# A gated mix of attention and a state-space convolution, backward pass: parameters prepared beside the projections, short-lag kernel gradient taken into the main channel loop

## The chip, the cores and the metric

The kernel runs on one core of one Trainium2 chip. The core has TensorE (PE, with its weight loads shown apart as PEld), VectorE (DVE), ScalarE (ACT), GpSimd (POOL) and SyncE (SP), which here issues the DMA transfers, in program order. The metric is the device time of one execution in microseconds (us), as the median of several runs.

## The reference

The reference computes the forward output and the gradients of all twelve differentiable inputs of a gated mix of two branches, for x of shape 1 x 2048 x 576:

```python
g = sigmoid((x * gate_w).sum(-1, keepdims=True))
a = attention(x, wqkv, wo)           # 32 heads of 18, softmax
# state-space branch, for each of 576 channels d with 128 states n:
dt = exp(log_dt)[:, None]
logdA = dt * (A_re + 1j * A_im)
P = exp(logdA[:, :, None] * arange(2048))
K = einsum("dn,dnl,dn->dl", Cc, P, dt * Bc).real
y = causal_convolution(x, K) + x * Dskip      # by FFT, length 4096
out = g * a + (1 - g) * y
out, vjp = jax.vjp(...); grads = vjp(grad_out)
```

Inputs and outputs are bf16.

## The kernel before

The sequence of 2048 tokens is 16 blocks of 128 (NB = 16), the 576 channels are five pieces of up to 128 (`dch`). The kernel has stages that follow one another:

- **Projections** (L84 to L212). x is transposed, q, k and v are projected for groups of four heads (`ps_proj`), scaled and stored. SyncE makes four transposes of `d_a` (the output gradient times the gate) for all 16 token tiles at L161. A loop over the 16 tiles (L201 to L212) then multiplies by wo transposed (`ps_dO`, ten matmuls) and evicts on VectorE and ScalarE in turn. `ps_dO` has one PSUM buffer.
- **Attention**, forward and backward, 230 to 2657 us, then the weight gradients, to 2870.8 us. The change does not touch them.
- **State-space parameters** (L604 to L720). 16 tiles of x are reversed by a matmul with `J_bf` and stored as `xr_d` (L636 to L643). The six parameter tensors are loaded by channel and transposed on PE (L658). From them come A times dt (`ath_d`, L676), the powers of the transition for a step of 1 and of 128 (`zpow`, L694) and 14 rows per channel, `par_d` (L720).
- **Short-lag kernel gradient** (L722 to L797): the part of dK for lags below 128. It is made from products of x with the gated output gradient inside each 16-token sub-block and up to seven sub-blocks back. For each of three batches of 192 channels, `xs` gets eight copies of x, each shifted by one more 16-token sub-block, by eight loads from DRAM (L765); partitions that would cross a block of 128 are set to zero by a mask (L767). `gyp` is the output gradient times 1 - g (L770), zero in its second half. A unit of 16 channels is 16 matmuls into `psM`, a copy to `mst` (L780), four stores to `Md_d` (L783) and two skewed loads back (`skw`, L789) with a matmul each that sums the diagonals into `dkp`. At the end `dkp` is copied to `DK` and its first row, the gradient of Dskip, to `dDs_d`. `xs`, `gyp` have two buffers each, `mst` three.
- **Main loop** (L799 to L986), 18 blocks of 32 channels; two blocks share what is loaded for 64. `load_rx` (L807) builds `RX`, the right-hand sides: x reversed, the gated gradient, both times their index, and the two columns of `DK`. `egen` (L819), twice per block for 16 channels each, loads `abuf` and `thb` (1 MB each; `thb` has one buffer) and computes the powers `E1e`; a DMA transpose on SyncE makes `E1n` of it (L873). 16 channels' `uvr` and `uvi` matmuls with E1e go to `UV`. VectorE runs a recurrence of 15 steps over the token blocks (`HG`, L888 to L896). GpSimd multiplies by a row of `par` (`wa` L912, `wb` L913, `Rw` L915, VectorE L916). `ybp` matmuls take E1n and Rw. VectorE's products `pA`, `pB`, `pC` (L942) are summed on PE into `smp`, and GpSimd finishes with small operations (L963). The kernel's first 128 lags go through `Kp_d` to `T0w` for the stage `t0_stage` (L841), which runs one block late.
- **Final** (from L988): the parameter gradients from sums over the states, the outputs.

A scheduler sets the order on each engine from the program's order and the buffers. SyncE issues each DMA in its place in that order: if one waits, all behind it wait.

Of the kernel before, what the change touches and what calls it, by code (L numbers as in the profile page):

```python
# [9 lines left out]
A = mybir.AluOpType  # L10
# [10 lines left out]
def build(tc, aps, dbg_aps=None, stages=("s1", "attn", "post", "s4", "final")):  # L21
# [39 lines left out]
    with ExitStack() as gctx:  # L61
# [24 lines left out]

        DPAD = DC * P
# [4 lines left out]
        with ExitStack() as ctx:  # L92
# [36 lines left out]
            go_tok = s1.tile([P, NT, D], BF, name="go_tok1")  # L129
            nc.sync.dma_start(go_tok, go_v)  # L130

# [22 lines left out]
            d_a = s1.tile([P, NT, DPAD], BF, name="d_a1")  # L154
            nc.gpsimd.memset(d_a[:, :, D:DPAD], 0.0)
            for t in range(NT):
                nc.vector.tensor_scalar(d_a[:, t, 0:D], go_tok[:, t, :], g_t[:, t:t + 1], None, op0=A.mult)
            for c in range(DC):
                nc.sync.dma_start_transpose(out=woT[:, :, c * P:(c + 1) * P], in_=wo_pad[:, c, :])
            d_aT = s1.tile([P, NT, DC, P], BF, name="d_aT")  # L160
            for tb in range(NBK):  # L161
                nc.sync.dma_start_transpose(out=d_aT[:, tb * TB:(tb + 1) * TB, :, :].rearrange("p t c q -> p (t c) q"),
                                            in_=d_a[:, tb * TB:(tb + 1) * TB, :].rearrange("p t d -> p (t d)"))

# [36 lines left out]
            for t in range(NT):  # L201
                psd = psB.tile([P, 2, 512], F32, tag="dO", bufs=1, name="ps_dO")
                for u, (f0, fsz) in enumerate(HALF):
                    for c, (e0, esz) in enumerate(dch):
                        mm(psd[:, u, 0:fsz], lhsT=d_aT[0:esz, t, c, :], rhs=woT[0:esz, c, f0:f0 + fsz],
                           start=(c == 0), stop=(c == DC - 1))
                dO_t = work.tile([P, D], BF, tag="dO_t", bufs=3, name="dO_t")
                if t % 2 == 0:
                    nc.vector.tensor_copy(dO_t.rearrange("p (u f) -> p u f", u=2), psd[:, :, 0:DH2])
                else:  # L210
                    nc.scalar.copy(dO_t.rearrange("p (u f) -> p u f", u=2), psd[:, :, 0:DH2])
                nc.sync.dma_start(dO_d[:, t, :], dO_t)  # L212

# [368 lines left out]
        if "s4" in stages:  # L582
            A_re = aps["B_A_re"]; A_im = aps["B_A_im"]; B_re = aps["B_B_re"]; B_im = aps["B_B_im"]
            C_re = aps["B_C_re"]; C_im = aps["B_C_im"]; log_dt = aps["B_log_dt"]; Dskip = aps["B_Dskip"]
            N = A_re.shape[1]
            NB = S // P
            NS = NB - 1
            SUB = 16
            NSUB = P // SUB
# [3 lines left out]
            NPAR = 14  # L593
            INV2PI = float(1.0 / (2.0 * np.pi))
            ath_d = dram.tile([2, D, N], F32, name="ath_d")
            par_d = dram.tile([P, NPAR, D], F32, name="par_d")
            omg_d = dram.tile([S], F32, name="omg_d")
            MW = P + SUB
            Md_d = dram.tile([D, SUB, MW], F32, name="Md_d")
            Kp_d = dram.tile([D, 2 * P], BF, name="Kp_d")  # L600
            yd_d = dram.tile([P, 2, NB, D], BF, name="yd_d")
            xr_d = dram.tile([P, NB, D], BF, name="xr_d")

            s4c_cm = tc.tile_pool(name="s4c", bufs=1)  # L604
            s4c = s4c_cm.__enter__()
            dt_b = s4c.tile([P, D], F32, name="dt_b")
            Ar_n = s4c.tile([P, D], BF, name="Ar_n"); Ai_n = s4c.tile([P, D], BF, name="Ai_n")
            Br_n = s4c.tile([P, D], BF, name="Br_n"); Bi_n = s4c.tile([P, D], BF, name="Bi_n")
            Cr_n = s4c.tile([P, D], BF, name="Cr_n"); Ci_n = s4c.tile([P, D], BF, name="Ci_n")
            S0r = s4c.tile([P, D], F32, name="S0r"); S0i = s4c.tile([P, D], F32, name="S0i")  # L610
            S1r = s4c.tile([P, D], F32, name="S1r"); S1i = s4c.tile([P, D], F32, name="S1i")
            DK = s4c.tile([P, 2, D], BF, name="DK")
            dDs_d = dram.tile([1, D], F32, name="dDs_d")
            nident_bf = s4c.tile([P, P], BF, name="nident_bf")
            nc.vector.tensor_scalar(nident_bf, ident_bf, -1.0, None, op0=A.mult)
# [8 lines left out]

            with ExitStack() as ctx:
                pp = ctx.enter_context(tc.tile_pool(name="s4pp", bufs=2))
                pp1 = ctx.enter_context(tc.tile_pool(name="s4pp1", bufs=1))
                pps = ctx.enter_context(tc.tile_pool(name="s4pps", bufs=2, space=bass.MemoryType.PSUM))
                with nc.allow_non_contiguous_dma(reason="gate values regrouped by 16 tokens"):
                    nc.sync.dma_start(omg_d.rearrange("(t p) -> p t", p=P), omg_t)  # L630
                DH2 = D // 2
                for t in range(NB):
                    x_t = pp.tile([P, D], BF, tag="x_t4", name="x_t4")
                    nc.sync.dma_start(x_t, x_v[:, t, :])
                    xr_t = pp.tile([P, D], BF, tag="xr_t4", name="xr_t4")
                    for u in range(2):  # L636
                        psr = pps.tile([P, DH2], F32, tag="psr", name="psr")
                        mm(psr, lhsT=J_bf, rhs=x_t[:, u * DH2:(u + 1) * DH2])
                        if u == 0:
                            nc.vector.tensor_copy(xr_t[:, 0:DH2], psr)  # L640
                        else:
                            nc.scalar.copy(xr_t[:, DH2:D], psr)
                    nc.sync.dma_start(xr_d[:, t, :], xr_t)  # L643
                zero_bf = pp1.tile([P, P], BF, name="zero_bf")
                nc.vector.memset(zero_bf, 0.0)
                for c, (d0, dsz) in enumerate(dch):
                    nc.sync.dma_start(Kp_d[d0:d0 + dsz, 0:P], zero_bf[0:dsz, :])
                tmpb = pp.tile([P, D], BF, tag="rowb", name="rowb")
                nc.sync.dma_start(tmpb, log_dt.rearrange("(o d) -> o d", o=1).to_broadcast([P, D]))
                nc.scalar.activation(dt_b, tmpb, ACT.Exp)  # L650
                cnt = 0
                for src_ap, dst in ((A_re, Ar_n), (A_im, Ai_n), (B_re, Br_n), (B_im, Bi_n), (C_re, Cr_n), (C_im, Ci_n)):
                    blk_ = pp.tile([P, DC, N], BF, tag="pblk", name="pblk")
                    for c, (d0, dsz) in enumerate(dch):
                        nc.sync.dma_start(blk_[0:dsz, c, :], src_ap[d0:d0 + dsz, :])
                    for c, (d0, dsz) in enumerate(dch):
                        pt = pps.tile([P, P], BF, tag="tp", name="pt_par")
                        nc.tensor.transpose(pt[:, 0:dsz], blk_[0:dsz, c, :], ident_bf[0:dsz, 0:dsz])  # L658
                        if cnt % 2 == 0:
                            nc.vector.tensor_copy(dst[:, d0:d0 + dsz], pt[:, 0:dsz])  # L660
                        else:
                            nc.scalar.copy(dst[:, d0:d0 + dsz], pt[:, 0:dsz])
                        cnt += 1
                    if src_ap is A_re or src_ap is A_im:
                        ltc = pp.tile([P, DC], BF, tag="ltc", name="ltc")
                        nc.gpsimd.memset(ltc, 0.0)
                        for c, (d0, dsz) in enumerate(dch):
                            nc.sync.dma_start(ltc[0:dsz, c:c + 1], log_dt.rearrange("(d o) -> d o", o=1)[d0:d0 + dsz, :])
                        dtc = pp.tile([P, DC], F32, tag="dtc", name="dtc")
                        nc.scalar.activation(dtc, ltc, ACT.Exp)  # L670
                        if src_ap is A_im:
                            nc.scalar.mul(dtc, dtc, INV2PI)
                        which_ = 0 if src_ap is A_re else 1
                        for c, (d0, dsz) in enumerate(dch):
                            sc_ = pp.tile([P, N], F32, tag="adn", name="adn")
                            nc.vector.tensor_scalar(sc_[0:dsz, :], blk_[0:dsz, c, :], dtc[0:dsz, c:c + 1], None, op0=A.mult)  # L676
                            nc.sync.dma_start(ath_d[which_, d0:d0 + dsz, :], sc_[0:dsz, :])

                def newt(nm):
                    return pp1.tile([P, D], F32, tag=nm, name=nm)  # L680

                def tt(o, a, b, op):
                    nc.vector.tensor_tensor(o, a, b, op=op)

                Wr_n = newt("Wr_n"); Wi_n = newt("Wi_n"); t1 = newt("t1")
                tt(Wr_n, Cr_n, Br_n, A.mult); tt(t1, Ci_n, Bi_n, A.mult)
# [32 lines left out]
                for r_, s_ in enumerate((Zr_n, Zr_n, Zr_n, Zr_n, Zi_n, Zi_n, nz, nz, wzr, wzi, zr_n, zi_n, nwr, nwi)):  # L719
                    nc.sync.dma_start(par_d[:, r_, :], s_)  # L720
# [447 lines left out]
```

## Time and profile before

| what | us |
|---|---|
| median of 3 runs (4868.92 to 4871.76) | 4869.47 |
| profiled execution | 4874.1 |
| its span | 4872.4 |
| projections, to attention's first matmul | 230.4 |
| start of the parameter stage | 2870.8 |
| start of the short-lag stage (memset of xs) | 2935.6 |
| start of the main loop (first RX load) | 3404.9 |
| first ybp matmul of the main loop | 3498.6 |

All of these are from the trace, but the first. A row of the windows table gives a stretch of the span: its length, the busy time and the number of instructions of each engine, the clock granted to TensorE, the share of time in which the DMA engines worked, and the bytes they moved. A row of the chain gives what ended last at each moment: an engine with its line, a DMA, or an engine's queue ("SPq") issuing. A group's row gives busy time, mean duration of one in ns, the idle time of the engine just before it, and what released it.

### The profile page before, as it was taken

How to read it: one execution, taken by the hardware profiler on the slowest of the kernel's cores; microseconds unless marked ns; L12 is line 12 of the kernel's file. 1: busy time of each engine (PE TensorE's matmuls, PEld its weight loads, DVE VectorE, ACT ScalarE, POOL GpSimd, SP SyncE). 2: the span in 40 equal slices, each digit the busy share in tenths (PEclk: the TensorE clock that was granted, in tenths of full speed). 3: DMA queues.
4: the chain of work that ended last, by engine and by line, in shares of the span. 5: the costliest groups of instructions: out<-in, count | busy, mean ns of one | idle time of the engine just before them, and what ended most of it. 6: DMA issues, size and time to landing. Idle time of an engine off the chain costs nothing. (4 is left out here: it accounts for less than half of the span.)

```text
span 4872.4 us, 64871 instructions
## 1 busy us (share of the span) xinstructions
PE 3174.3 (65%) x24304; PEld 1144.3 (23%) x24304; DVE 3011.4 (62%) x5252; ACT 2883.8 (59%) x5068; POOL 528.1 (11%) x747
## 2 busy tenths in 40 slices
PE   8899999999999999999997870222122122222121
PEld 2222222222222222222222440111122121122110
DVE  4267677776777777777776221001677666667768
ACT  4399899898998989899895110000444433443411
POOL 0000000000000000000000003000243343344320
PEclk9755555555555555555555975555555555555555
DMA  6357767777677676786768752223544544454347
GB/s 172 100 93 125 135 120 125 136 125 135 120 124 139 124 135 120 129 133 120 129 119 164 197 146 86 68 59 76 148 108 102 129 108 114 108 115 114 102 99 177
DMA packets 1761726, 594.16 MB, mean 122 GB/s; under 512 B 1679615, under 2 KB 1732033, under 8 KB 1752195
## 3 DMA queue, kind: packets, MB, share of 16 engines
q1 hardware_dynamic: 1761410, 590.02, 58.8%
q8 instruction: 191, 3.13, 0.3%
q14 instruction: 125, 1.02, 0.1%
HBM read 193.30 MB, written 59.49 MB: 52 GB/s over the span
## 5 line engine op out<-in xcount | busy, mean ns | idle before, releaser
L478 DVE TENSOR_TENSOR ds<-ps_P,PT 128x512 bf16<-128x512 f32 x2048 | 1329.3, 687 | 468.6 <-PE ps_P L30 262.5
L469 ACT ACTIVATE PT<-ps_P 128x512 bf16<-128x512 f32 x2048 | 1226.4, 603 | 138.7 <-PE ps_P L30 86.8
L473 ACT ACTIVATE eb<-ps_P 128x512 bf16<-128x512 f32 x2048 | 1236.1, 605 | 19.9 <-PE ps_P L30 19.4
L30 PE MATMUL ps_P<-dOaT,VaT_g 19*128 19x512 bf16 x2048 | 1197.7, 601 | 27.1 <-DMA VaT_g<-VaT_d 26.2
L30 PE MATMUL ps_P<-KaT_g,QaT_g 19*128 19x512 bf16 x2048 | 1165.4, 593 | 7.6 <-ACT PT L469 7.6
L30 PE MATMUL ps_P<-QaT_g,KaT_g 19*128 19x512 bf16 x2048 | 1053.7, 615 | 10.1 <-DMA KaT_g<-KaT_d 6.1
L30 PE MATMUL uvr<-RX,E1e 128*128 128x64 bf16 x576 | 72.4, 291 | 655.3 <-DVE E1e L834 655.3
L30 PE MATMUL accO<-PT,Vtok_g 128*32 128x512 bf16 x2048 | 331.5, 631 | 0.0
L30 PE MATMUL accK<-dsT,Qtok_g 128*32 128x256 bf16 x4096 | 315.1, 406 | 1.7 <-DVE dqa L355 0.8
L30 PEld LDWEIGHTS <-VaT_g 19*128 19x128 bf16 x2048 | 197.4, 98 | 434.7 <-issue 404.8
L30 PEld LDWEIGHTS <-KaT_g 19*128 19x128 bf16 x2048 | 135.6, 103 | 690.7 <-issue 664.9
L30 PEld LDWEIGHTS <-E1e 128*128 128x128 bf16 x1152 | 119.7, 123 | 731.8 <-DVE E1e L834 636.6
L780 ACT COPY mst<-psM 128x512 f32<-128x512 f32 x36 | 21.9, 609 | 440.3 <-PE psM L30 364.6
L30 PE MATMUL accQ<-ds,Ktok_g 128*32 128x512 bf16 x2048 | 266.9, 620 | 1.2 <-DVE dvacc L338 1.2
L30 PE MATMUL accV<-eb,dOa 128*32 128x512 bf16 x2048 | 267.0, 620 | 0.6 <-DVE dkacc L379 0.6
L499 POOL MEMSET O_tok<- 128x1024 bf16 x1 | 1.0, 957 | 2429.3 <-DMA dqkv_d<-dtk 2429.3
L767 DVE TENSOR_SCALAR xs<-xs,msk 128x3072 bf16<-128x3072 bf16 x21 | 21.4, 1020 | 379.3 <-DMA xs<-in_A_x_dram 379.3
L30 PE MATMUL psM<-xs,gyp 128*32 128x128 bf16 x576 | 54.7, 550 | 261.2 <-DVE xs L767 189.1
L826 ACT ACT_TABLE_LOAD x35 | 44.9, 1283 | 297.1 <-DMA abuf<-ath_d 296.9
L30 PE MATMUL ybp<-Rw,E1n 128*128 128x31 bf16 x1152 | 71.2, 233 | 224.9 <-POOL Rw L915 219.5
L30 PEld LDWEIGHTS <-QaT_g 19*128 19x128 bf16 x2048 | 178.8, 100 | 51.7 <-issue 28.0
L355 DVE TENSOR_TENSOR dqa<-dqa,accQ 128x512 f32<-128x512 f32 x224 | 153.8, 687 | 48.9 <-PE accQ L30 48.6
(300 smaller groups left out, 4436.3 us busy)
## 6 DMA issues: line engine op xcount, KB each, us to landing
abuf<-ath_d SPq DMA_DIRECT2D x36, 1024.0 KB
thb<-ath_d SPq DMA_DIRECT2D x36, 1024.0 KB
T0w<-Kp_d SPq DMA_DIRECT2D x36, 512.0 KB
dsT<-ds SPq DMA_TRANSPOSE x512
dqkv_d<-dtk SPq DMA_DIRECT2D x96, 72.0 KB
dqkv_tok<-dqkv_d SPq DMA_DIRECT2D x1, 6912.0 KB
Md_d<-mst SPq DMA_DIRECT2D x144, 36.0 KB
ga_d<-ga_st SPq DMA_DIRECT2D x16, 288.0 KB
```

Source lines behind the costliest of these rows:

```text
L30: return nc.tensor.matmul(out, lhsT=lhsT, rhs=rhs, start=start, stop=stop, **kw)
L355: nc.vector.tensor_tensor(U["dqa"], U["dqa"], acc, op=A.add)
L469: nc.scalar.activation(U["PT"][i][:, j, :], ps, ACT.Exp)
L473: nc.scalar.activation(e, ps, ACT.Exp)
L478: nc.vector.tensor_tensor(U["ds"][i][:, j, :], ps, U["PT"][i][:, j, :], op=A.mult)
L499: nc.gpsimd.memset(O_tok[:, :, D:DPAD], 0.0)
L767: nc.vector.tensor_scalar(xs[:, dl, :, :], xs[:, dl, :, :], msk[:, dl:dl + 1], None, op0=A.mult)
L780: nc.scalar.copy(mst[:, :, 0:P], psM)
L826: nc.scalar.activation(abuf, abuf, ACT.Exp, scale=l0col)
```

## The change

The parameter stage moves into the projection stage; `xr_d` is made there from `x_pad`, behind the `dO` loop, with the same single PSUM buffer, and a DMA transpose replaces the transposes on PE. The output gradient and `d_aT` are made there for four tiles at a time, with two buffers, instead of for all 16. The short-lag stage is gone. Its work is four functions that the main loop calls for 64 channels at a time, one pair of blocks ahead; the first 64 channels are done ahead of the loop. `xs` is loaded once from DRAM (256 KB) and shifted seven times by DMAs within SBUF. `xs` and `gyp` have one buffer. `dkp` goes straight into `RX`.

Buffers of the loop change with it: `uvr` and `uvi` share three PSUM buffers (two each before), E1n comes in halves of 16 channels with three buffers, `wa` and `wb` take the buffers of `pA` and `pB`, `rr` has one buffer instead of two, and the first kernel block is transposed in f32 into a part of `smp`. The final stage loads `dt_b` and the six parameters (`prm5`) from DRAM.

```diff
+                    go_b = work.tile([P, TB, D], BF, tag="go_b", name="go_b")
+                    nc.sync.dma_start(go_b, go_v[:, t:t + TB, :])
...
+                    d_aT = work.tile([P, TB, DC, P], BF, tag="d_aT", name="d_aT")
+                    nc.sync.dma_start_transpose(out=d_aT.rearrange("p t c q -> p (t c) q"), in_=d_a.rearrange("p t d -> p (t d)"))
...
+            for t in range(NT):
+                psr = psB.tile([P, 2, 512], F32, tag="dO", bufs=1, name="psr")
+                for u in range(2):
+                    mm(psr[:, u, 0:DH2], lhsT=J_bf, rhs=x_pad[:, t, u * DH2:(u + 1) * DH2])
...
+                pr_ = s1.tile([P, DC, P], BF, name=f"prm{r_}")
+                nc.sync.dma_start_transpose(out=pr_, in_=blk_.rearrange("p c n -> p (c n)"))
...
+                nc.sync.dma_start(prm_d[:, r_, :], pr_)
...
-                    for dl in range(NSUB):
-                        nc.sync.dma_start(xs[dl:P, dl, :, :], xsub[0:P - dl, :, d0:d0 + DB])
...
+                def m_load(xb):
...
+                    nc.sync.dma_start(xs[:, 0, :, :], xsub[:, :, d0:d0 + XB])
...
+                    nc.sync.dma_start(gyp[:, 0:SUB, :], gsub[:, :, d0:d0 + XB])
+                    for dl in range(1, NSUB):
+                        nc.sync.dma_start(xs[dl:P, dl, :, :], xs[0:P - dl, 0, :, :])
+                    nc.vector.tensor_tensor(gyp[:, 0:SUB, :], gyp[:, 0:SUB, :], omp.unsqueeze(2).to_broadcast([P, SUB, XB]), op=A.mult)
+                    for dl in range(1, NSUB):
+                        nc.vector.tensor_scalar(xs[:, dl, :, :], xs[:, dl, :, :], msk[:, dl:dl + 1], None, op0=A.mult)
...
+                def m_fin(xb):
...
+                    nc.vector.tensor_copy(dDs_row[:, xb * XB:(xb + 1) * XB], pk[0:1, :])
+                    nc.scalar.copy(RX[:, CDK, :], pk)
+                    nc.vector.tensor_scalar(RX[:, CDK + 1, :], pk, l0col, None, op0=A.mult)
...
+                m_load(0)
+                load_rx(0)
+                for u in range(4):
+                    m_part(0, u)
+                    m_sum(0, u)
+                m_fin(0)
                 for b in range(D // CB):
...
-                        load_rx(d0 // XB)
+                        if nxt < NXB:
+                            m_load(nxt)
...
+                        E1n_h = pw.tile([P, GS, 2, P], BF, tag="E1n", bufs=3, name="E1n")
...
-                            pr = pps.tile([P, NCOL, 8], F32, tag="uvr", bufs=2, name="uvr")
-                            pi = pps.tile([P, NCOL, 8], F32, tag="uvi", bufs=2, name="uvi")
+                            pr = pps.tile([P, NCOL, 8], F32, tag="uv", bufs=3, name="uvr")
+                            pi = pps.tile([P, NCOL, 8], F32, tag="uv", bufs=3, name="uvi")
...
+                    if nxt < NXB:
+                        if b % 2 == 0:
+                            m_part(nxt, 0)
+                            m_part(nxt, 1)
+                        else:
+                            load_rx(nxt)
+                            m_sum(nxt, 0)
+                            m_sum(nxt, 1)
+                            m_part(nxt, 2)
+                            m_part(nxt, 3)
...
-                        wa = pw.tile([P, 2, NS, CB], F32, tag="wa", bufs=1, name="wa")
-                        wb = pw.tile([P, 2, NS, CB], F32, tag="wb", bufs=1, name="wb")
+                        wa = pw.tile([P, 2, NS, CB], F32, tag="pA", bufs=1, name="wa")
+                        wb = pw.tile([P, 2, NS, CB], F32, tag="pB", bufs=1, name="wb")
...
+                    if nxt < NXB and b % 2 == 1:
+                        m_sum(nxt, 2)
+                        m_sum(nxt, 3)
+                        m_fin(nxt)
...
+                dt_b = pf.tile([P, D], F32, name="dt_b5")
+                nc.sync.dma_start(dt_b, dt_d)
+                prm5 = pf.tile([P, 6, D], BF, name="prm5")
+                nc.sync.dma_start(prm5, prm_d)
```

`m_part` and `m_sum` are the old unit of 16 channels (the 16 matmuls, the copy and the four stores; then the two skewed loads with their matmuls), cut in two.

SyncE at the start of the main loop, before: from the first RX load to the first E1n transpose and the second thb load.

```order
L810 DMA RX<-xr_d 128x16x64
L812 DMA gob<-in_grad_out_dram 128x16x64
L868 DMA par<-par_d 128x14x32
L823 DMA abuf<-ath_d 128x2048
L824 DMA thb<-ath_d 128x2048
L823 DMA abuf<-ath_d 128x2048
L868 DMA par<-par_d 128x14x32
L810 DMA RX<-xr_d 128x16x64
L812 DMA gob<-in_grad_out_dram 128x16x64 x2
L873 DMA_TRANSPOSE E1n<-E1e 128x32x128
L824 DMA thb<-ath_d 128x2048
```

The same engine now, the rows just ahead of the first E1n transpose (L784 and L786 are the loads of `m_load`, L788 its shifts, L807 a store of `m_part`, L818 a load of `m_sum`).

```order
L818 DMA skw<-Md_d 128x1x128 x2
L807 DMA Md_d<-mst_39351 16x4x144 x2
L784 DMA xs_39345<-in_A_x_dram 128x16x64
L786 DMA gyp_39347<-in_grad_out_dram 128x16x64
L818 DMA skw<-Md_d 128x1x128 x2
L788 DMA xs_39345<-xs_39345 127x1024
L788 DMA xs_39345<-xs_39345 126x1024
L788 DMA xs_39345<-xs_39345 125x1024
L788 DMA xs_39345<-xs_39345 124x1024
L788 DMA xs_39345<-xs_39345 123x1024
L788 DMA xs_39345<-xs_39345 122x1024
L788 DMA xs_39345<-xs_39345 121x1024
```

The next two rows are E1n and thb: they have moved behind the stores and loads of the first four units and behind the second load with its seven shifts.

SyncE some blocks into the loop, before:

```order
L933 DMA Kp_d<-KT 32x128
L845 DMA T0w<-Kp_d 128x16x128 x2
L868 DMA par<-par_d 128x14x32
L873 DMA_TRANSPOSE E1n<-E1e 128x32x128
L824 DMA thb<-ath_d 128x2048
L823 DMA abuf<-ath_d 128x2048
L873 DMA_TRANSPOSE E1n<-E1e 128x32x128
```

And now:

```order
L963 DMA Kp_d<-KT 32x128
L788 DMA xs_39345<-xs_39345 121x1024
L853 DMA T0w<-Kp_d 128x16x128 x2
L885 DMA par<-par_d 128x14x32
L807 DMA Md_d<-mst_39349 16x4x144
L735 DMA RX<-xr_d 128x16x64
L807 DMA Md_d<-mst_39349 16x4x144 x3
L807 DMA Md_d<-mst_39351 16x4x144 x2
L892 DMA_TRANSPOSE E1n<-E1e 128x32x128
L864 DMA yd_d<-yd 4096x1x64
L832 DMA thb<-ath_d 128x2048
```

Stores of `mst` and shifts of `xs` stand between the loads of a block and its transpose.

ScalarE in the projection stage, before (L181 and L179 evict projections, L194 is a square root):

```order
L181 ACTIVATE stg<-ps_proj,onec 128x512 x6
L179 ACTIVATE stg<-ps_proj 128x512 x2
L194 ACTIVATE sh<-ps_884,kmxg 128x512
L194 ACTIVATE sh<-ps_898,kmxg 128x512
L179 ACTIVATE stg<-ps_proj 128x512 x2
```

And now (L193, L191 and L206 are the same three; L310 and L311 are sines of `zpow`):

```order
L310 ACT_TABLE_LOAD
L310 ACTIVATE gk<-gv 128x576
L191 ACTIVATE stg<-ps_proj 128x512
L206 ACT_TABLE_LOAD
L206 ACTIVATE sh<-ps_872,kmxg 128x512
L206 ACTIVATE sh<-ps_886,kmxg 128x512
L206 ACTIVATE sh<-ps_900,kmxg 128x512
L191 ACTIVATE stg<-ps_proj 128x512
L193 ACTIVATE stg<-ps_proj,onec 128x512
L311 ACT_TABLE_LOAD
L311 ACTIVATE gv<-gv 128x576
```

The activations of the parameters, with loads of their table and back, stand between the square roots and evictions.

More of the change, by code (lines that the diff above doesn't have):

```diff
@@ L204, in build @@
                     for c, (e0, esz) in enumerate(dch):
-                        mm(psd[:, u, 0:fsz], lhsT=d_aT[0:esz, t, c, :], rhs=woT[0:esz, c, f0:f0 + fsz],
+                        mm(psd[:, u, 0:fsz], lhsT=d_aT[0:esz, t % TB, c, :], rhs=woT[0:esz, c, f0:f0 + fsz],
                            start=(c == 0), stop=(c == DC - 1))
@@ new lines, in build @@
+            zero_bf = s1.tile([P, P], BF, name="zero_bf")
+            nc.vector.memset(zero_bf, 0.0)
+            for c, (d0, dsz) in enumerate(dch):
+                nc.sync.dma_start(Kp_d[d0:d0 + dsz, 0:P], zero_bf[0:dsz, :])
+            dt_b = s1.tile([P, D], F32, name="dt_b")
+            tmpb = work.tile([P, D], BF, tag="rowb", bufs=1, name="rowb")
+            nc.sync.dma_start(tmpb, log_dt.rearrange("(o d) -> o d", o=1).to_broadcast([P, D]))
+            nc.scalar.activation(dt_b, tmpb, ACT.Exp)
@@ new lines, in build @@
+            nc.sync.dma_start(dt_d, dt_b)
+            ltc = s1.tile([P, DC], BF, name="ltc")
+            nc.gpsimd.memset(ltc, 0.0)
+            for c, (d0, dsz) in enumerate(dch):
+                nc.sync.dma_start(ltc[0:dsz, c:c + 1], log_dt.rearrange("(d o) -> d o", o=1)[d0:d0 + dsz, :])
+            dtc = s1.tile([P, DC], F32, name="dtc")
+            nc.scalar.activation(dtc, ltc, ACT.Exp)
+            dtci = s1.tile([P, DC], F32, name="dtci")
+            nc.scalar.mul(dtci, dtc, INV2PI)
@@ L582, in build @@
         if "s4" in stages:
[L583 to L589, printed above, removed]
             CB = 32
@@ new lines, in m_part @@
+                def m_part(xb, u):
+                    d0 = xb * XB
+                    xs = xs2[xb % 2]
+                    gyp = gy2[xb % 2]
+                    psM = pps.tile([P, 4, P], F32, tag="psM", name="psM")
+                    for q in range(4):
+                        for g_ in range(4):
+                            dd = u * 16 + 4 * q + g_
+                            mm(psM[32 * g_:32 * (g_ + 1), q, :].rearrange("p (a b) -> p a b", b=SUB), lhsT=gyp[:, :, dd],
+                               rhs=xs[:, :, ::-1, dd], tile_position=(0, 32 * g_))
+                    mst = mst2[u % 2]
+                    nc.scalar.copy(mst[:, :, 0:P], psM)
+                    for g_ in range(4):
+                        dst = Md_d[d0 + u * 16:d0 + (u + 1) * 16].rearrange("(q g) t w -> g t q w", g=4)
+                        nc.sync.dma_start(dst[g_], mst[32 * g_:32 * g_ + SUB, :, :])
@@ new lines, in m_sum @@
+                def m_sum(xb, u):
+                    d0 = xb * XB
+                    if u == 0:
+                        dkps[xb] = pps.tile([P, XB], F32, tag="dkp", name="dkp")
+                    for v in range(2):
+                        o = u * 16 + v * 8
+                        skw = pw.tile([P, P], F32, tag="skw", bufs=3, name="skw")
+                        src = bass.AP(tensor=Md_d.tensor, offset=Md_d[d0 + o:d0 + o + 1, 0:1, SUB - 1:SUB].offset,
+                                      ap=[[SUB * MW, 8], [MW - 1, SUB], [1, P]])
+                        nc.sync.dma_start(skw, src)
+                        mm(dkps[xb][:, o:o + 8], lhsT=skw, rhs=sel)
```

364 lines of the change are left out of this document (157 added, 207 removed).

## The prediction

> **What bounds the kernel now.** I read the page first, then the windows table cut at the borders of the stages, then the chain of waits of the stretch that the change removes.
>
> ```profile
> span 4872.4 us, 64871 instructions
> ```
>
> The profiled execution took 4874.1 us, 1.7 us more than its span, and lies 4.6 us above the median of the three runs (4869.47 us). The sum below starts from 4874.1 and takes 4.6 off at the end.
>
> The windows table (columns: length, busy time and count on PE, PEld, DVE, ACT, POOL, then the clock, the DMA share, GB/s):
>
> ```profile
> 0.00:230.40 230.40, 192.28 (x784) 67.51 (x784) 87.86 (x186) 83.10 (x125) 10.69 (x29) 0.90 0.46 130
> 2870.80:2935.60 64.80, 17.82 (x62) 5.47 (x62) 33.73 (x80) 15.98 (x42) 0.29 (x5) 0.53 0.54 166
> 2935.60:3404.90 469.30, 93.50 (x720) 62.65 (x720) 34.22 (x38) 22.63 (x38) 46.82 (x10) 0.54 0.27 66
> 3404.90:3498.60 93.70, 11.63 (x96) 10.14 (x97) 56.94 (x87) 42.24 (x34) 14.13 (x11) 0.54 0.61 153
> 3640.00:3780.00 140.00, 31.95 (x482) 29.11 (x483) 98.32 (x179) 58.77 (x57) 49.58 (x69) 0.52 0.46 113
> 4708.00:4872.40 164.40, 21.73 (x146) 9.31 (x144) 124.95 (x251) 25.55 (x48) 0.32 (x2) 0.50 0.68 172
> ```
>
> Row 1 is the projection stage: PE is the engine that sets it, ACT and DVE have more than half of it free. Row 2 prepares the state-space parameters, row 3 is the short-lag kernel gradient. In row 3 no engine is busy for a fifth of the time, and the DMA engines work for 0.27 of it: it is waiting. Row 4 runs from the start of the main loop to its first ybp matmul. Row 5 is one steady 64-channel pair of main-loop blocks: DVE is busy 98 of 140 us, nothing is full. From 2870.8 to the first ybp matmul at 3498.6 it is 627.8 us.
>
> What row 3 waits for, in the chain of waits from 2870 to 3500 (start, length, what):
>
> ```profile
> 2935.63 20.50 POOL xs L747
> 2958.08 38.32 SPq L765
> ...
> 3028.33 26.74 DMA xs<-in_A_x_dram
> ...
> 3246.90 76.69 DMA xs<-in_A_x_dram x3
> ```
>
> The shifted loads (eight of about 760 KB for each third of the channels) and SyncE's time to issue them are the stage. After them its units of 16 channels run one behind another.
>
> **The change: what is taken away.** A stretch of 627.8 us is replaced by one that holds only the first 64 channels' gradient and the loop's own start. The price of its pieces comes from these rows, the units first (timeline), then two landings (chain):
>
> ```profile
> 3067.52 1.63 PE L30 MATMUL psM<-xs,gyp 128*32 128x128 bf16 x16 [0.48 <-ACT mst L780]
> ...
> 3068.12 1.88 SPq L783 DMA_DIRECT2D Md_d<-mst  x4
> ...
> 3070.55 1.22 SPq L789 DMA_DIRECT2D skw<-Md_d  x2
> ...
> 3071.30 1.62 PE L30 MATMUL psM<-xs,gyp 128*32 128x128 bf16 x16 [0.89 <-ACT mst L780]
> ```
> ```profile
> 3060.14 2.72 DMA Md_d<-mst
> ...
> 3075.20 2.55 DMA skw<-Md_d
> ```
> ```profile
> L780 ACT COPY mst<-psM 128x512 f32<-128x512 f32 x36 | 21.9, 609 | 440.3 <-PE psM L30 364.6 <-DMA Md_d<-mst 50.5 <-PE dkp L30 25.2
> ```
>
> One unit alone: 1.6 + 0.6 + 1.9 + 2.7 + 1.2 + 2.6 = 10.6 us; units in a row follow each other by 3.8 us (3067.5 to 3071.3). Four take 10.6 + 3 x 3.8 = 22 us.
>
> How the loop starts now, on SyncE and on VectorE:
>
> ```profile
> 3404.90 0.56 SPq L810 DMA_DIRECT2D RX<-xr_d  x1
> ...
> 3411.31 6.10 SPq L810 DMA_DIRECT2D RX<-xr_d  x1
> ...
> 3431.57 4.98 SPq L873 DMA_TRANSPOSE E1n<-E1e  x1
> 3436.64 0.53 SPq L824 DMA_DIRECT2D thb<-ath_d  x1
> ```
> ```profile
> 3408.95 0.47 DVE L815 TENSOR_SCALAR RX<-RX,l1col 128x960 bf16<-128x960 bf16 x1 [3.65 <-DMA RX<-xr_d]
> 3410.75 1.23 DVE L813 TENSOR_TENSOR RX<-gob,omg_t 128x1024 bf16<-128x1024 bf16 x1 [1.33 <-DMA gob<-in_grad_out_dram]
> ...
> 3417.09 1.28 DVE L827 TENSOR_SCALAR uk<-thb,l0col 128x2048 f32<-128x2048 f32 x1 [4.61 <-DMA thb<-ath_d]
> ```
> ```profile
> 3498.60 1.60 PE L30 MATMUL ybp<-Rw,E1n 128*128 128x31 bf16 x26 [12.72 <-POOL Rw L915]
> ```
>
> From the second thb issue (3436.6) to the first ybp it is 62.0 us, and I keep that. In the new order the first E1n and second thb stand behind the whole first gradient block and the shifts of the second. With T = 2870.8: the 2.8 MB up to thb landed in 12.2 us (3404.9 to 3417.1), 230 GB/s; the new xs load has 2.2 MB with and before it (10 us), and the set-up of masks and zeros stands ahead, so xs is there at T+18. Seven shifts within SBUF move 1.75 MB, which no row of this trace shows. Lower end: at 230 GB/s 7.6 us; upper end: three old shift loads held SyncE 38.3 us for 2.25 MB, so 30 us. I take 10, nearer the low end, because a shift now moves one 2 KB row per partition and one start address. The seven masks (128x1024) cost 0.5 each as L815, all but the last beside the shifts, and the gyp product 1.2 as L813: T+31. Four units: T+53. The second block's xs reload waits for the first block's last psM matmuls (T+44), its seven shifts are issued behind the last skw, 4 to 10 us (a single DMA held SyncE for 6.1 us above), then E1n 5.0: second thb at T+62 to T+72, taken T+68. First ybp at T+130, a gain of 627.8 - 130 = **498 us**. Bounds: T+94 if nothing on SyncE is late (31.7 + 62), T+152 with the slow shifts.
>
> **What is added ahead: the projection stage.**
>
> ```profile
> 217.62 2.89 PE L30 MATMUL ps_dO<-woT,d_aT 128*128 128x288 bf16 x10 [0.73 <-ACT dO_t L211]
> 221.41 2.90 PE L30 MATMUL ps_dO<-woT,d_aT 128*128 128x288 bf16 x10 [0.91 <-DVE dO_t L209]
> 230.44 0.62 PE L30 MATMUL ps_P<-QaT_g,KaT_g 19*128 19x512 bf16 x4 [6.13 <-DMA KaT_g<-KaT_d]
> ```
>
> The 16 reversed x tiles follow the last dO step, in the same single PSUM buffer. A step is 2 matmuls of this shape, 2.9 x 2/10 = 0.58, and an eviction gap of 0.73 or 0.91: 1.40 x 16 = **+22 us**, all on PE's path, with the same 6 us to attention behind it. The parameter work (30 some VectorE operations, 15 activations, over 60 DMAs on SyncE) has cover: DVE and ACT are idle for 140 us of row 1. But it stands in line ahead of evictions that PE waits for. ACT's functions now alternate, with nine more table loads. In the loop one looks like this:
>
> ```profile
> 3601.31 2.00 ACT L826 ACTIVATE abuf<-abuf,l0col 128x2048 f32<-128x2048 f32 x1
> 3603.33 1.28 ACT L830 ACT_TABLE_LOAD   x1
> 3604.63 1.91 ACT L830 ACTIVATE uk<-thb 128x2048 f32<-128x2048 f32 x1
> ```
>
> From the end of one activation (3603.31) to the start of the next it is 1.32 us, so nine are 12 us of ACT's time. PE has three PSUM buffers of projection ahead, so only pairs of load and activation that fall together reach it: **+4 us**, between 0 and 12.
>
> The Trainium skill (ScalarE: Activation LUTs, What ACT_TABLE_LOAD costs) counts a drain of about 1.38 us to each switch, 2.66 us in all. By that the nine would be 24 us, and an estimate from it puts the term at 8 instead of 4. The rows above show no such drain.
>
> **What is added to the loop.** Per pair, from row 5 and these:
>
> ```profile
> L30 PE MATMUL uvr<-RX,E1e 128*128 128x64 bf16 x576 | 72.4, 291 | 655.3 <-DVE E1e L834 655.3
> ```
> ```profile
> 3484.42 1.21 POOL L912 TENSOR_TENSOR wa<-HG,par 128x480 f32<-128x480 f32 x1 [71.81 <-DVE HG L895]
> 3485.59 1.66 POOL L913 TENSOR_TENSOR wb<-HG,par 128x480 f32<-128x480 f32 x1
> 3487.21 1.19 POOL L912 TENSOR_TENSOR wa<-HG,par 128x480 f32<-128x480 f32 x1
> ```
> ```profile
> L942 DVE TENSOR_TENSOR pA<-UV,hR 128x960 bf16<-128x960 bf16 x36 | 41.7, 1177 | 10.6 <-ACT hR L901 10.6
> ```
>
> The 16 uvr matmuls of a half block (72.4/36 = 2.0 us) now alternate with uvi, so they no longer run beside E1e's second operation: 1.5 us a block, +3 a pair (0 to 4). The pA and pB products share buffers with POOL's wa and wb and wait until these are read: the four operations of a block (4 x 1.2 us) leave POOL's shadow, pC and the masks take their place: +3 (0 to 10). POOL in turn runs more of its steps undisturbed (1.2 instead of 1.66): -3. Masks and gyp: 7 x 0.5 + 1.2, mostly in VectorE's waits: +1. DMA: shifts 1.75 MB, xs and gyp 0.5, Md_d and skw 1.1, so 3.35 MB on the pair's 15.8 MB (140 us at 113 GB/s); the share goes from 0.46 to about 0.56, which lengthens the abuf and thb loads: +4 (0 to 8). SyncE: 16 stores (0.47), 8 skw (0.61), 9 loads and shifts, 18 us of issue and the round trips behind which E1n and thb stand; what covers it is SyncE's wait at E1n:
>
> ```profile
> SPq L873 <- DVE E1e L835: 175.4, 9, 21.5
> SPq L873 <- DVE tz L892: 145.9, 9, 24.9
> ```
>
> 16 to 19 us each time in these rows. Much of it stays hidden: +3 (0 to 10). In all **+11 us a pair** (0 to 25), times 8.3 pairs behind the first ybp: **+91 us** (0 to 207).
>
> **The end.** dt_b and prm5 (1.2 MB) are loaded ahead of the last stage, which moves 172 GB/s (row 6): 1.2/0.172 = 7 us, of which I count **+5**.
>
> Sum: 4874.1 - 498 + 22 + 4 + 91 + 5 = 4498, less 4.6: 4494, called **4495 us**.
>
> **The rivals.** First, the loop takes the gradient for nothing (+0 a pair): row 5 speaks for it, with 42 us of VectorE and half of the DMA time free; against it, that loads come in bursts. 4495 - 91 = 4404 us, chance 0.24.
>
> Second, the loop becomes bound by transfers: bursts of shifts in front of thb, which has one buffer, +30 a pair: 4495 + 19 x 8.3 = 4653 us, chance 0.13. The Trainium skill (DMA: Bandwidth & Descriptors, Why small descriptors are slow (HBM only)) puts the loss on short pieces read from HBM, not on copies within SBUF; by it the shifts would be cheap and the xs and gyp loads, now in 128-byte pieces instead of 384, dear. The RX load, cut the same way, landed within 4.1 us of its issue here (3404.9 to 3408.95).
>
> Third, the work is only relocated: the parameter stage's 64.8 us reappear in full in the projection stage, because ACT and SyncE there are in order: +65 instead of +26, 4534 us, chance 0.06.
>
> Fourth, slower than before: each unit's round trip (10.6 us) and the shifts (10 to 30 us) stand in SyncE's line one after another between two E1n, 4 x 10.6 + 30 = 72 us a pair, and nothing of it is covered. 4495 + 61 x 8.3 = 5001 us. It decides from 56 us a pair on ((498 - 31)/8.3). Against it: the 16 to 19 us of wait at each of four E1n a pair. Chance 0.02.
>
> **How the numbers follow.** My forecast has 0.55. The range 4400 to 4600 us holds it with its bounds, the first and the third rival, some 0.85. A measurement of this kernel can tell 0.2%, about 10 us, from no change. Only the fourth rival is near or above 4870: faster 0.97, same 0.01, slower 0.02.
>
> **What would show it.** Right: no stretch without VectorE between the output-projection gradient and the loop; first ybp about 130 us after it; second thb issued some 68 us in; attention's first matmul at about 256 us; pairs of 151 us. Wrong: first ybp past 152 us or before 94, pairs under 143 or over 165, E1n transposes that wait for SyncE's line instead of E1e, or PE gaps over 5 us within the projections.

## The result and the profile after

The changed kernel takes 4519.93 us (median of 4 runs, 4516.95 to 4521.86), the kernel before 4870.61 us beside it: a ratio of 0.928 (95% interval 0.926 to 0.929). The forecast was 4495 us, with a range of 4400 to 4600.

The page's first row, after:

```profile
span 4520.1 us, 64796 instructions
```

To see where the 352.3 us between the two profiled spans come from, I cut both traces at the same four events: the end of the last weight-gradient matmul (`ps_dwo`), the first eviction of ybp, the last one, and the end. The windows tables (first number: length), before and after:

```profile
2870.79:3500.57 629.78, 124.92 (x918) 80.24 (x918) 126.24 (x207) 80.85 (x114) 61.23 (x24) 0.54 0.34 89
3500.57:4698.00 1197.43, 277.89 (x4255) 253.21 (x4252) 839.43 (x1523) 485.98 (x481) 440.25 (x663) 0.53 0.46 109
4698.00:4872.40 174.40, 25.87 (x249) 13.04 (x245) 127.56 (x258) 26.76 (x52) 6.50 (x28) 0.52 0.67 169
```
```profile
2890.14:3063.07 172.93, 38.35 (x324) 28.93 (x328) 73.02 (x132) 46.95 (x45) 13.87 (x15) 0.54 0.56 137
3063.07:4345.46 1282.39, 357.02 (x4761) 300.50 (x4761) 853.39 (x1579) 483.80 (x504) 434.60 (x663) 0.53 0.50 119
4345.46:4520.10 174.64, 27.66 (x265) 13.91 (x265) 128.76 (x260) 26.76 (x52) 6.50 (x28) 0.50 0.69 175
```

| stretch | before | after | difference | forecast |
|---|---|---|---|---|
| up to the last weight-gradient matmul | 2870.8 | 2890.1 | +19.4 | +26 |
| from there to the first ybp eviction | 629.8 | 172.9 | -456.9 | -498 |
| first to last ybp eviction | 1197.4 | 1282.4 | +85.0 | +91 |
| the rest | 174.4 | 174.6 | +0.2 | +5 |

The projection stage: the reversed tiles (`psr`) on TensorE and the first attention matmul, after.

```profile
218.13 2.90 PE L30 MATMUL ps_dO<-woT,d_aT 128*128 128x288 bf16 x10 [0.90 <-DVE dO_t L230]
221.76 0.64 PE L30 MATMUL psr<-x_pad,J_bf 128*128 128x288 bf16 x2 [0.73 <-ACT dO_t L232]
223.25 0.64 PE L30 MATMUL psr<-x_pad,J_bf 128*128 128x288 bf16 x2 [0.85 <-DVE xr_t L244]
...
243.46 0.64 PE L30 MATMUL psr<-x_pad,J_bf 128*128 128x288 bf16 x2 [0.85 <-DVE xr_t L244]
250.25 0.62 PE L30 MATMUL ps_P<-QaT_g,KaT_g 19*128 19x512 bf16 x4 [6.16 <-DMA KaT_g<-KaT_d]
```

The 16 steps take 22.3 us (221.76 to 244.10), as forecast. The last dO step starts at 218.13 instead of 221.41, so no net delay of the projections shows in this run.

The start of the main loop, on SyncE, after:

```profile
2906.46 18.54 SPq L788 DMA_DIRECT2D xs<-xs  x7
...
2959.41 18.50 SPq L788 DMA_DIRECT2D xs<-xs  x7
2978.01 10.99 SPq L892 DMA_TRANSPOSE E1n<-E1e  x1
2989.05 0.57 SPq L832 DMA_DIRECT2D thb<-ath_d  x1
```

Seven shifts within SBUF hold SyncE for 18.5 us, and the E1n transpose behind them takes 11 us where it took 5. The second thb leaves at 2989.05, 98.9 us after the last weight-gradient matmul; the prediction had 68. From there to the first ybp matmul (3061.1) it is 72 us instead of 62.

When the second set of shifts lands is seen at the masks, which VectorE runs as they come in:

```profile
2972.99 0.49 DVE L791 TENSOR_SCALAR xs<-xs,msk 128x1024 bf16<-128x1024 bf16 x1 [10.36 <-DMA xs<-xs]
2973.73 0.49 DVE L791 TENSOR_SCALAR xs<-xs,msk 128x1024 bf16<-128x1024 bf16 x1 [0.25 <-DMA xs<-xs]
2975.72 0.49 DVE L791 TENSOR_SCALAR xs<-xs,msk 128x1024 bf16<-128x1024 bf16 x1 [1.51 <-DMA xs<-xs]
2978.20 0.49 DVE L791 TENSOR_SCALAR xs<-xs,msk 128x1024 bf16<-128x1024 bf16 x1 [1.99 <-DMA xs<-xs]
2981.54 0.49 DVE L791 TENSOR_SCALAR xs<-xs,msk 128x1024 bf16<-128x1024 bf16 x1 [2.86 <-DMA xs<-xs]
2986.45 0.49 DVE L791 TENSOR_SCALAR xs<-xs,msk 128x1024 bf16<-128x1024 bf16 x1 [4.42 <-DMA xs<-xs]
2987.34 0.48 DVE L791 TENSOR_SCALAR xs<-xs,msk 128x1024 bf16<-128x1024 bf16 x1 [0.40 <-DMA xs<-xs]
```

The steps between them are 0.7, 2.0, 2.5, 3.3, 4.9 and 0.9 us, for nearly equal transfers of 252 to 242 KB over 126, 125, 124, 123, 122 and 121 partitions. The kernel before has the same pattern in its loads from DRAM (second batch, 126 to 122 partitions):

```profile
3147.09 1.02 DVE L767 TENSOR_SCALAR xs<-xs,msk 128x3072 bf16<-128x3072 bf16 x1 [2.42 <-DMA xs<-in_A_x_dram]
3154.54 1.02 DVE L767 TENSOR_SCALAR xs<-xs,msk 128x3072 bf16<-128x3072 bf16 x1 [6.43 <-DMA xs<-in_A_x_dram]
3164.52 1.02 DVE L767 TENSOR_SCALAR xs<-xs,msk 128x3072 bf16<-128x3072 bf16 x1 [8.96 <-DMA xs<-in_A_x_dram]
3176.84 1.02 DVE L767 TENSOR_SCALAR xs<-xs,msk 128x3072 bf16<-128x3072 bf16 x1 [11.30 <-DMA xs<-in_A_x_dram]
3195.36 1.02 DVE L767 TENSOR_SCALAR xs<-xs,msk 128x3072 bf16<-128x3072 bf16 x1 [17.50 <-DMA xs<-in_A_x_dram]
```

Here 125, 124, 123 and 122 take 7.5, 10.0, 12.3 and 18.5 us. The largest divisors up to 16 of these four numbers are 5, 4, 3 and 2, and time by divisor is 37, 40, 37 and 37 us: nearly constant. In the new kernel the same products are 10.0, 9.9, 10.0 and 9.8 us, and 126 and 121, with 14 and 11, give 10.4 and 9.8. So the theory that the runs were made for (A): a transfer is spread over as many DMA engines as the largest number up to 16 that divides its partition count; 127 has 1. One engine then moves about 25 KB per us (half of the 244 KB of 122 partitions in 4.9 us), and the 254 KB over 127 partitions need about 10 us; they landed 13.6 us after SyncE began the set (2959.41 to 2972.99), and the whole set 27.9 us after.

### The profile page after: what moved, and what is told of

Same layout as the page of the kernel before. It is cut to its first block, busy times and chain, and to the rows that moved or that the text cites. A ratio compares the mean times of both kernels' runs of the same rounds, so it can differ in the third digit from the quotient of the medians.

```text
span 4520.1 us, 64796 instructions
## 1 busy us (share of the span) xinstructions
PE 3174.4 (70%) x24274; PEld 1144.6 (25%) x24274; DVE 2998.5 (66%) x5286; ACT 2869.0 (63%) x5049; POOL 475.8 (11%) x746
## 5 line engine op out<-in xcount | busy, mean ns | idle before, releaser
L30 PE MATMUL uvr<-RX,E1e 128*128 128x64 bf16 x576 | 99.9, 290 | 293.3 <-DVE E1e L842 292.5
L941 POOL TENSOR_TENSOR wa<-HG,par 128x480 f32<-128x480 f32 x72 | 99.8, 1386 | 772.8 <-DVE HG L924 769.7
L459 DVE TENSOR_TENSOR dvacc<-dvacc,accV 128x512 f32<-128x512 f32 x224 | 154.2, 688 | 37.1 <-PE accV L30 18.4
L30 PE MATMUL dkp<-sel,skw 128*128 128x8 f32 x144 | 37.9, 362 | 194.3 <-DMA skw<-Md_d 155.2
```

The costliest lines, as they stand in the source:

```text
L30: return nc.tensor.matmul(out, lhsT=lhsT, rhs=rhs, start=start, stop=stop, **kw)
L459: nc.vector.tensor_tensor(a_, a_, acc, op=A.add)
L941: nc.gpsimd.tensor_tensor(wa[:, ri], hv[:, ri], par[:, 8, :].unsqueeze(1).to_broadcast([P, NS, CB]), op=A.mult)
```

## The experiments

All times are medians of four executions (split at a prime: two). The kernel before took 4872.22 us beside split shifts, no shifts, no short-lag gradient and before with split loads, and 4870.98 us beside the other four experiments. "Start" is from the last weight-gradient matmul to the first ybp eviction, "loop" from first to last ybp eviction, as in the table above, both from one profiled execution. What lies ahead of the start is not quite the same in all: the last weight-gradient matmul ends at 2890.1 us in the changed kernel and between 2887.0 and 2899.8 in its seven variants, so the totals of these differ by some us that their edits do not explain, and starts and loops are compared.

| run | us | start | loop |
|---|---|---|---|
| changed kernel | 4519.9 | 172.9 | 1282.4 |
| split shifts | 4438.5 | 133.1 | 1234.6 |
| split at a prime | 4790.9 | 260.0 | 1464.6 |
| no shifts | 4417.2 | 111.3 | 1233.6 |
| no short-lag gradient | 4375.4 | 99.9 | 1198.0 |
| split, no masks | 4416.5 | 130.2 | 1219.3 |
| split, no sums | 4411.4 | 131.4 | 1209.8 |
| sub-block-major | 4421.7 | 121.5 | 1229.3 |
| before, loads split | 4671.9 | 429.7 | 1191.7 |
| before | 4870.6 | 629.8 | 1197.4 |

**Split shifts.** The changed kernel with

```diff
-                        nc.sync.dma_start(xs[dl:P, dl, :, :], xs[0:P - dl, 0, :, :])
+                        nc.sync.dma_start(xs[dl:dl + 112, dl, :, :], xs[0:112, 0, :, :])
+                        nc.sync.dma_start(xs[dl + 112:P, dl, :, :], xs[112:P - dl, 0, :, :])
```

> Each of the seven shifts inside SBUF (127 to 121 partitions) is cut in two: 112 partitions, and the 9 to 15 left. The bytes are the same, the transfers are 14 instead of 7. Theory A (few engines: a transfer is spread over as many DMA engines as the largest number up to 16 that divides its partition count, so 127 go over one, 126 over 14, 125 over 5, 124 over 4, 123 over 3, 122 over 2, 121 over 11, and what is queued behind waits for the first of them): SyncE's 18.5 us for a set of shifts fall to 7 to 9 us, the first E1n transpose takes 5 us instead of 11, the first ybp comes 125 to 135 us after the last weight-gradient matmul instead of 171, the loop from first to last ybp takes about 1245 us instead of 1284, the run about 4440 us. Theory B (copies within SBUF are slow by themselves, or SyncE pays for each descriptor): no gain, 4515 to 4530 us.

SyncE at the second set, with the transpose behind it:

```profile
2943.33 0.61 SPq L788 DMA_DIRECT2D xs<-xs  x1
2943.99 0.86 SPq L789 DMA_DIRECT2D xs<-xs  x1
...
2952.81 0.77 SPq L789 DMA_DIRECT2D xs<-xs  x1
2953.68 4.94 SPq L893 DMA_TRANSPOSE E1n<-E1e  x1
2958.66 0.58 SPq L833 DMA_DIRECT2D thb<-ath_d  x1
```

Fourteen transfers are issued in 10.3 us (7 to 9 were expected), the transpose is back at 4.9. The ratio to the kernel before is 0.911 (0.909 to 0.912), 4438.5 us where theory A said 4440. The start falls by 40 us, the loop by 48. Theory B is out: the copies are as much within SBUF as before, and twice as many.

**Split at a prime.** The same two transfers per shift, cut at 113 partitions instead of 112.

```diff
+                        nc.sync.dma_start(xs[dl:dl + 113, dl, :, :], xs[0:113, 0, :, :])
+                        nc.sync.dma_start(xs[dl + 113:P, dl, :, :], xs[113:P - dl, 0, :, :])
```

> The same cut in two, but at 113 partitions instead of 112, and 7 to 14 left: the same number of transfers and bytes, but 113 has no divisor up to 16 but 1. Theory A (engines by divisor): seven transfers of 226 KB go over one engine at 20 to 21 GB/s, 11 us each, 77 us a set instead of 5; SyncE stands for most of it, first ybp 210 to 250 us after the last weight-gradient matmul, the run 4650 to 4900 us. If the split helped for any other reason (smaller transfers, more of them in flight): about 4440 us.

SyncE in the second set:

```profile
3046.60 0.63 SPq L788 DMA_DIRECT2D xs<-xs  x1
3047.28 8.04 SPq L789 DMA_DIRECT2D xs<-xs  x1
3055.41 10.33 SPq L893 DMA_TRANSPOSE E1n<-E1e  x1
```

One partition more in the large piece makes it 4790.9 us, 352 us more than at 112. From the second 113-partition shift on, the issue behind it is held for 8 to 9 us; at the 25 KB per us above, 226 KB over one engine are 9 us, and the 11 that were expected came from the slower old loads. The set holds SyncE from 2997.2 to 3055.3. The start is some 8 us beyond what was expected, the run within. This is the cleanest evidence that the partition count decides: size, number and direction of the transfers are the same to 1%. That it goes by the largest divisor, and not only by multiples of 16, rests on the ratios of the steps above.

**Before, loads split.** The kernel before, its shifted loads from DRAM cut at 112 in the same way.

```diff
+                        nc.sync.dma_start(xs[dl:dl + 112, dl, :, :], xsub[0:112, :, d0:d0 + DB])
+                        nc.sync.dma_start(xs[dl + 112:P, dl, :, :], xsub[112:P - dl, :, d0:d0 + DB])
```

> The kernel before, with its shifted loads from DRAM cut in the same way (112 partitions and the rest). Theory A: a 762 KB load takes 2 to 4 us instead of up to 37, the short-lag stage shrinks from 469 us to 200 to 230 us (its 36 units at 3.8 us and the set-up), the run takes about 4610 us: more than half of what the change gained was this. Theory B: the loads are slow because they come in pieces of 384 bytes, so the stage stays within 30 us and the run within 4840 to 4870 us.

The masks of the second batch:

```profile
3049.51 1.02 DVE L768 TENSOR_SCALAR xs<-xs,msk 128x3072 bf16<-128x3072 bf16 x1 [54.17 <-DMA xs<-in_A_x_dram]
3052.57 1.02 DVE L768 TENSOR_SCALAR xs<-xs,msk 128x3072 bf16<-128x3072 bf16 x1 [2.04 <-DMA xs<-in_A_x_dram]
3055.74 1.02 DVE L768 TENSOR_SCALAR xs<-xs,msk 128x3072 bf16<-128x3072 bf16 x1 [2.15 <-DMA xs<-in_A_x_dram]
```

The seven of this batch land 3.1 to 3.9 us apart instead of 3.4 to 18.5. The run takes 4671.9 us, a ratio of 0.959 (0.957 to 0.960): 200 us of the 351 that the change gained are to be had in the old order by cutting the loads. I had expected 260; the stage is 268 us long, not 200 to 230. With the transfers cut in both, the changed kernel is still 233 us faster (4671.9 to 4438.5): that is what the new order itself is worth. The stage still waits 54 us between batches, since the next loads stand on SyncE behind the twelve units before.

**No shifts.** The changed kernel without its seven transfers.

```diff
-                    nc.vector.memset(xs_u[0:NSUB], 0.0)
+                    nc.vector.memset(xs_u, 0.0)
...
-                    for dl in range(1, NSUB):
-                        nc.sync.dma_start(xs[dl:P, dl, :, :], xs[0:P - dl, 0, :, :])
```

> The changed kernel without the seven shift transfers of each 64 channels (the shifted copies are zeros, so the products of different sub-blocks are left out of the short-lag gradient); the masks stay. It is the floor of what any repair of the shifts can reach. Theory A: 5 to 20 us below the run with the split shifts, about 4425 us. Theory B: the same 4425 us, while the split run stays at 4520. If the loop's extra time is not the shifts at all but the units' round trips in SyncE's line (rival C): 4490 us or more.

4417.2 us, 21 below the split run where 5 to 20 were expected. The loop is 1233.6 us, against 1234.6 with split shifts: cut in two the shifts cost the loop next to nothing, only 22 us at the start. Uncut they cost it 49. Rival C, that only the units' round trips matter, is out as the whole cause.

**No short-lag gradient.** All calls of `m_load`, `m_part`, `m_sum` and `m_fin` are taken out, here the first of them:

```diff
+                    nc.vector.memset(RX[:, CDK:CDK + 2, :], 0.0)
...
-                m_load(0)
...
-                    m_part(0, u)
-                    m_sum(0, u)
-                m_fin(0)
```

> The changed kernel without the short-lag kernel gradient altogether (its two columns and the gradient of Dskip are zeros); all other edits of the loop stay. It prices the loop's other edits (shared PSUM buffers, products that wait for GpSimd, single rr). By the prediction's terms of +3 us a pair for these: first ybp 94 us after the last weight-gradient matmul, loop from first to last ybp 1224 us, the run about 4383 us. If these edits cost nothing: loop 1199 us, 4358 us. If they are the whole of the loop's +85 us: loop 1284 us, 4443 us.

Its loop:

```profile
2999.65:4197.69 1198.04, 286.64 (x4233) 253.81 (x4232) 817.68 (x1524) 464.38 (x467) 441.60 (x663) 0.52 0.44 109
```

1198.0 us, the kernel before 1197.4. The other edits of the loop (three shared PSUM buffers for uvr and uvi, products behind GpSimd's reads, one rr) cost nothing together; +3 a pair, 25 us in all, was wrong. So the loop's 85 us are the short-lag work: 48 for the narrow shifts, 37 for the rest. That these edits cost something only beside the short-lag work is not ruled out by a run. The total of 4375.4 us is above the 4358 that went with this case, 9.6 us of it ahead of the start (2899.8 against 2890.1).

**What the 37 us are.** Two runs, each from the split version: without the masks, and without the skewed loads and their matmuls.

```diff
-                        nc.vector.tensor_scalar(xs[:, dl, :, :], xs[:, dl, :, :], msk[:, dl:dl + 1], None, op0=A.mult)
```

> The split shifts, without the seven mask operations of each 64 channels (products that cross a block of 128 tokens then stay in the short-lag gradient). With split shifts the loop takes 1234.6 us from first to last ybp's eviction, 37 us more than with no short-lag work (1198.0). Theory D (VectorE's time: 7 masks of 0.49 us and a product of 1.2 us a pair, eight pairs, are 37 us by themselves): the loop falls by 20 to 27 us, to about 1210, the run to about 4408 us. Theory E (round trips: TensorE's and SyncE's lines wait for the stores to Md_d and the skewed loads back): the loop stays above 1228 us, the run above 4428.

```diff
-                    m_sum(0, u)
...
-                            m_sum(nxt, 0)
-                            m_sum(nxt, 1)
...
-                        m_sum(nxt, 2)
-                        m_sum(nxt, 3)
```

> The split shifts, without the skewed loads and the matmuls that sum them (the two columns and the gradient of Dskip are zeros); shifts, masks, products, copies and stores to Md_d stay. Theory E: the loop falls from 1234.6 to 1205 us or less, the run to about 4400 us. Theory D: the loop stays at 1228 us or more, the run at 4425 or more (the start is some 5 to 10 us shorter, since nothing waits for the sums).

Neither theory got its number. Without masks the loop is 15 us shorter (1219.3), without sums 25 (1209.8). What the sums hold up is seen in the waits over the loop (us in total, times, longest), TensorE and VectorE with split shifts:

```profile
PE dkp L30 <- DMA skw<-Md_d: 112.0, 26, 19.0
```
```profile
DVE HG L918 <- ACT UV L905: 70.7, 10, 13.0
```

And VectorE without the sums:

```profile
DVE HG L913 <- ACT UV L902: 40.7, 11, 9.7
```

TensorE stands at `dkp` for the skewed loads, up to 19 us, with uvr and uvi of the next block behind it; VectorE's recurrence then waits for UV, 71 us instead of 41. These waits speak for E, on TensorE's line; no run took the wait off TensorE and left the loads on SyncE's. The masks are seven operations of 0.49 us for each 64 channels, 27 us for the eight sets behind the first, of which some 15 show. The two together are 40 us where 37 were to be explained, so they overlap or the order of the engines shifts by as much.

**A version to beat both.** Partitions hold the 16-token sub-blocks ordered by (place within the block of 128, block) instead of (block, place).

```diff
+                    nc.sync.dma_start(dst_[s_ * SUB:(s_ + 1) * SUB, :, :], src_.rearrange("(b s t) d -> s b t d", s=NSUB, t=SUB)[s_])
...
-                        nc.sync.dma_start(xs[dl:P, dl, :, :], xs[0:P - dl, 0, :, :])
+                        nc.sync.dma_start(xs[SUB * dl:P, dl, :, :], xs[0:P - SUB * dl, 0, :, :])
...
-                        nc.vector.tensor_scalar(xs[:, dl, :, :], xs[:, dl, :, :], msk[:, dl:dl + 1], None, op0=A.mult)
```

> A version to beat both: partitions hold the sub-blocks in the order (sub-block within its block, block) instead of (block, sub-block). A shift by one sub-block is then a move by 16 partitions that never crosses a block: no masks, and seven transfers of 112, 96, ... 16 partitions, all multiples of 16. x and the output gradient are copied once to DRAM in that order, early. Theory A and D: 4395 to 4410 us. Theory A and E: 4425 to 4435 us.

```profile
2938.36 4.44 SPq L787 DMA_DIRECT2D xs<-xs  x7
2942.90 5.45 SPq L889 DMA_TRANSPOSE E1n<-E1e  x1
```

4421.7 us, 0.908 (0.906 to 0.909) of the kernel before and 98 us below the changed one. The set is issued in 4.4 us and the start is 121.5 us. The time lies between the two ranges, above the 4410 that was hoped for: the loop is 1229.3 us, 5 us below the split one, although it has no masks either, while the split one without masks is 15 below. The order that the scheduler gives all engines differs between these kernels; which place makes the 10 us was not tried.

## Why the prediction was right, and where it was not

The main step held: the two stages were waiting and not work, and 457 of the forecast 498 us of the stretch went. What the waiting came from, the prediction did not see. That the total came within 25 us has luck in it: the start fell 41 us short of its forecast, while the projections, the loop and the end came out 7, 6 and 5 us below theirs. Point by point:

- **Projection stage, +22 and +4.** The reversed tiles: 22.3 us measured. The +4 for ScalarE's interleaved tables does not show. There are ten more table loads ahead of attention (12 against 2); TensorE waits for ScalarE's eviction of a projection once, 1.04 us at 117.40, and that eviction stood behind an `sh` that had itself waited for TensorE; the kernel before has one such wait of 0.8 us. A switch there and back, ScalarE, after:

```profile
117.24 0.69 ACT L193 ACTIVATE stg<-ps_proj,onec 128x512 bf16<-128x512 f32 x1
117.95 1.28 ACT L311 ACT_TABLE_LOAD   x1
119.25 0.69 ACT L311 ACTIVATE gv<-gv 128x576 f32<-128x576 f32 x1
119.95 1.28 ACT L206 ACT_TABLE_LOAD   x1
121.24 0.69 ACT L206 ACTIVATE sh<-ps,kmxg 128x512 bf16<-128x512 f32 x1
```

  From the end of one activation (117.93) to the next (119.25) it is 1.32 us. The drain of 1.38 us that the Trainium skill adds to each switch (ScalarE: Activation LUTs, What ACT_TABLE_LOAD costs) is not seen here, so its estimate of 8 us was further off than the row's 4. The third rival (the stage's 65 us only moved) is out: +19.4. A term of 4 us can hardly be judged here: the first attention matmul starts at 250.3 us in the changed kernel, and between 245.1 and 257.9 in its variants, six of which leave the code of the projections as it is.
- **Start of the loop, T+130.** This step failed: 171 to the first ybp matmul, beyond the bound of 152. It failed in "Seven shifts within SBUF ... I take 10, nearer the low end": a set holds SyncE for 18.5 us and lands in 28, twice ahead of the second thb, and lengthens the transpose and the thb behind it. The upper end, 30 us, came from the old shift loads, and was right because they had the same fault, the partition count. I read those loads as slow by their bytes and pieces, and the row of 38.3 us as three of them; in the trace it is the issue of a single load (the third, begun at 2958.08), held behind the one over 127 partitions. By theory A that one is 762 KB over one engine, 38 us at the 20 KB per us of the rows above. The bound of 152 lies 22 us above the forecast, about one slow set, where two stood ahead. With the shifts cut in two, the second thb leaves 67.7 us in (68 forecast), and the start is 133.1 us to the first eviction, about 131 to the first matmul: the rest of that step was sized well.
- **Loop, +11 a pair, +91.** +85.0 measured, by other terms. Edits of buffers and order: 0 instead of 3 a pair. DMA and SyncE together were 7 a pair, 58 us in all; in their place stand the 48 us of narrow shifts, and 25 us by the run without the sums, which its waits put on TensorE's line, a place that I had not named. Masks: some 15 us instead of 8. The sum was close because errors of both signs met, which is luck. The second rival had bursts of shifts in front of thb at +30 a pair; the narrow shifts cost about 6.
- **Blocks are uneven.** The prediction spoke of pairs of 151 us. The scheduler runs the short-lag work ahead: from one ybp to the next it is 89 to 98 us in four of the blocks with shifts, and 62 to 79 us behind the last shifts (3677 us). Pairs run from 134 to 187 us, outside the 143 to 165 that it gave as a sign of being wrong: one price per pair was not how the loop paid.
- **The end, +5:** +0.2. The two loads cost nothing that shows; no run tells what covers them.

The Trainium skill names the rule that was missed: DMA: Bandwidth & Descriptors, Why a DMA increments its semaphore by 16 and not by 1, says that a transfer from SyncE uses the largest number of engines up to 16 that divides the slowest dimension on both sides, and gives 127 partitions as 1. The rows agree: 125 to 122 partitions take times in the ratio of 1/5, 1/4, 1/3 and 1/2. What I cited instead, that copies within SBUF do not suffer from small pieces, is neither shown nor refuted here, since the pieces were 2 KB.

## What to carry to other kernels

Look at the partition count of each transfer before its size: by these runs a shifted copy of 128 - k partitions can go over one engine, and what stands behind it in the queue is late too, even for another buffer. Cut it at a multiple of 16 (112), or lay out the partitions so that shifts are multiples of 16. Where an old stage is slow because of a wait, find out why before it is hidden under other work: cutting the old loads alone gave 200 us where the change gave 351, and the moved work took the fault along.

## What the runs showed of the hardware that I had not expected

- By theory A, one DMA engine moved about 20 GB/s on the old loads in 384-byte pieces (732 KB over 2 engines in 18.5 us) and 25 GB/s on 2 KB rows within SBUF (244 KB over 2 in 4.9 us).
- A slow transfer over few engines delays one behind it: the issue of an E1n transpose held SyncE for 4.9 us behind shifts cut at 112, for 11.0 behind the uncut ones and for 10.3 behind those cut at 113.
- One partition (113 instead of 112) made the whole kernel 8% slower.
